# A new instruction order for a fused attention and feed-forward layer

## The chip, the cores and the metric

The kernel runs on one core of one Trainium2 chip. Such a core has five engines, each with an instruction queue of its own that it works through in order: TensorE (PE in the profile) multiplies matrices, VectorE (DVE), ScalarE (ACT) and GpSimd (POOL) work element by element, and SyncE (SP) here only issues DMAs. ScalarE issues some DMAs too, from the same queue as its arithmetic. Matrix products land in PSUM, eight banks of 512 fp32 columns, and are copied out ("evacuated") by VectorE or ScalarE.

The metric is the time on the device, in microseconds (us), median of the runs shown.

## The reference

One pre-norm transformer layer over 2048 tokens of width 640, with 32 heads of 20. Attention goes in four segments of 512 tokens: each segment has causal softmax attention within itself, and a linear memory of the segments before it, mixed by a gate from beta. A feed-forward part of width 1728 with silu follows.

```python
for s in range(N):                      # N = 4 segments of L = 512
    qs, ks, vs = q[:, :, s], k[:, :, s], v[:, :, s]
    p = softmax(qs @ ks.T * scale + mask)
    a_dot = p @ vs
    a_mem = (phi(qs) @ M) / (phi(qs) @ z + 1e-06)
    outs.append(g * a_mem + (1 - g) * a_dot)
    M, z = M + phi(ks).T @ vs, z + phi(ks).sum()
h = x + concat(outs) @ wo               # q, k, v from layernorm(x)
out = h + silu(layernorm(h) @ w1) @ w2
```

Here phi(t) is t + 1 for positive t, and exp(t) otherwise.

## The kernel before

The program is a graph of many small tasks. `ORDER`, a list of names, gives the order in which they are emitted; `schedule` (L287) reads it. An entry such as `n1_st3/A:0,0` is a task, the engine that it goes to (A ScalarE, D VectorE, G GpSimd, S SyncE, where the task may go to more than one) and the buffer slots that it takes. The list is the outcome of a search over a model of the chip; the model's costs are not in the program. Each engine gets its own tasks in the order of the list, so the list is five queue orders at once; waits between engines are worked out from the data (`Tracker.add`, L91).

Every task name has a stage and numbers. In the order of the data, for segment s, 128-token block b (four a segment), head group g of four heads and chunk c of 128 columns:

- `x0`, `x1`, `x2` (blocks 2 and 3), `x4` (blocks 4 to 7), `x8` (8 to 11), `x12`: loads of the tokens (L579). `w_q`, `w_k0`, `w_k1`, `w_wv0`, `w_wv1`, `w_wo`, `w_w1_*`, `w_w2_*`: loads of the weights (L582); `beta` (L594).
- `n1_st`, `n1_r`, `n1_ap`: layer norm of a block, as statistics (L747, L750; on ScalarE L739, L742), one over the deviation (an addition, L762 on VectorE or L765 on GpSimd, then a power on GpSimd, L768) and application (L774). In segment 0 `n1_tp` transposes on TensorE (L783) and `n1_te` evacuates (L792); later `n1_tr` is a transposing DMA (L798). `n2_*` is the second layer norm.
- `re_wq`, `re_wk`: copies that put the query and key weights' columns in order (L699).
- `pr` (L861): query (w = 0) and key (w = 1) projections of chunk c, in segment 0 in two halves x and y; `qe` evacuates them (L869 on ScalarE, L870 on VectorE). `ex` (L876), `pha` (L883) and `phb` (L889) make phi.
- `vt` (L901): twelve small DMAs a segment that move parts of the chunks 0 to 4 to other partitions, for the head groups 5 to 7. They are issued from SP and ScalarE.
- `v` (L826) and `ve` (L836, L837): values. `qk` (L938): scores of four heads; `e` (L949): their exponential on ScalarE; `mk` (L960): the causal mask of a diagonal block, on GpSimd.
- `av` (L981): scores times values; `oe` (L994, L996): evacuation; `tn` (L1010, L1014): memory part and transpose; `nm` (L1027 to L1047): normalization; `ad` (L1055): sum. `kt` (L1095), `mz` (L1103), `ma`, `mb` (L1129 to L1139): the memory.
- `ot` (L1156), `wo` (L1164), `rs` (L1172): output projection and residual. `h1` (L1193, L1199), `th` (L1208), `s` (L1214): the first feed-forward product and silu; `h2` (L1241), `o` (L1254), `out` (L1259): the second product, residual and store.
- `zpad` is a tile of zeros, `sel` the identity (L633, from `iota`), `w2z` and `vpad0`, `vpad1` are memsets on GpSimd, `mt`, `mta`, `mtb`, `mm`, `mzc` small constants there. `fill36` is 36 matmuls on zeros without use for the result (L619), and needs `zpad`. `zf0` and `lsc0` read beta on ScalarE.

Of the kernel before, what the change touches and what calls it, by code (L numbers as in the profile page):

```python
# [371 lines left out]
mk3x_256 phb041 vt04/S vt05/S vt08/S pr010y:6 pr020y:7 pha021:1 qe010y/D lsc2 qe020y/D pr011y:5 qe011y/D lsc3 pr000y:4  # L372
qe000y/D n1_st11:2 ex021:0 phb021 n1_r11/D qk4x0:0 e4x2:5 v00:6 e4x0 mk4x_0 ve00/D:0 n1_st9:1 n1_ap5:0 mk4x_256
n1_r9/D vt03/A n1_ap11:1 vt00/S vt09/S qk0yb0:2 e0yb2:4 v01:0 e0yb0 mk0yb_0 vt06/A ve01/A ex011:2 mk0yb_256 vt010/S
n1_tr5 n1_tr4 kt00:1 kt02:0 n1_tr7 w_w1_1 v03:6 ve03/D qk1yb0:2 e1yb0:6 av0x:0 av2x:1 oe0x/D:1 av4x:6 oe2x/D:0 e1yb2
mk1yb_0 mk1yb_256 tn0x:7 nm0x:0 n1_st10:0 n1_r10/D oe4x/A:1 n1_ap9:0 qk7x0:0 v02:4 e7x2:2 e7x0 mk7x_0 tn4x:7 mk7x_256
ve02/A av1x:6 oe1x/D:1 n1_ap10:2 qk5x0:0 e5x0:0 e5x2 mk5x_0 nm4x:0 v11:4 pha011:2 phb011 qk6x0:0 mk5x_256 ve11/D:1
tn2x:7 av7x:6 ex031:0 e6x2:1 oe7x/D:0 tn1x:4 e6x0 mk6x_0 mk6x_256 nm1x:3 fill2:5 av3x:5 nm2x:1 tn7x:6 nm7x:2 oe3x/A:1
qk0ya0:0 e0ya2:5 av5x:4 oe5x/D:0 mz00:5 ma00/D:0 mb00:0 tn3x:7 nm3x:1 e0ya0 av6x:6 qk1ya0:2 kt04:1 e1ya2:0 oe6x/D:1
tn5x:7 nm5x:3 tn6x:6 nm6x:0 pha031:1 phb031 ot1:0 n1_st8:6 ot0 e1ya0 n1_r8/G v10:0 ve10/A qk2ya0:4 e2ya0:2 av0y:3  # L380
oe0y/D:1 mz02:2 ma02/D:3 v12:0 e2ya2 qk2yb0:2 e2yb0:1 mb02:0 w_w2_0/A e2yb2 mk2yb_0 ve12/D wo1:6 qk3ya0:0 e3ya2:3
kt01:0 rs1 mk2yb_256 n2_st1:5 n2_r1/G wo0:4 tn0y:6 nm0y:1 rs0 e3ya0 n2_ap1:3 n2_tr1:0 av1y:7 oe1y/A:0 qk4ya0:0 pr101:6
v13:4 e4ya2:4 e4ya0 qe101/D:0 n2_st0:3 n2_r0/G ve13/D pha101:2 n2_ap0:3 n2_tr0 ex101:2 phb101 qk3yb0:0 e3yb2:5 pr120:7
qe120/D:0 e3yb0 mk3yb_0 mk3yb_256 qk4yb0:2 e4yb0:0 e4yb2 mk4yb_0 av2y:6 oe2y/D:1 mk4yb_256 w_w2_1/S ex120:0 pr100:0
qe100/D qk5ya0:2 e5ya2:2 tn2y:6 nm2y:2 e5ya0 pr121:1 pha120:0 phb120 qk5yb0:4 e5yb0:6 qe121/D pha121:0 e5yb2 n1_ap8:3
pr141:0 qe141/D:0 qk6ya0:1 h1_0_7_0:5 av3y:6 tn1y:7 mk5yb_0 pha100:0 nm1y:1 e6ya0:1 th0_7_0:0 s0_7_0:0 oe3y/D:1
h1_0_5_0:0 e6ya2 th0_5_0:1 h1_0_12_0:1 th0_12_0:0 qk7ya0:2 e7ya2:3 mk5yb_256 av5y:7 s0_5_0 s0_12_0 oe5y/D:0 mz01:6
e7ya0 tn3y:0 ma01/D:2 mb01:0 nm3y:0 kt03:0 h1_0_4_0:1 qk6yb0:4 e6yb2:5 e6yb0 mk6yb_0 mk6yb_256 pr110:0 qe110/D:0
th0_4_0:0 ex100:1 h1_0_3_0:2 s0_4_0 pha110:0 th0_3_0:1 s0_3_0 phb100 qk7yb0:4 w_w2_2/S w_w2_3/S e7yb2:2 av4y:3
oe4y/D:1 e7yb0 mk7yb_0 ex121:2 pr140:0 qe140/D h1_0_1_0:1 th0_1_0:1 mk7yb_256 pha140:0 s0_1_0 qk8a0:2 e8a0:6 tn4y:6  # L390
# [926 lines left out]
```

## Time and profile before

| | |
|---|---|
| Median of 3 runs | 301.52 us (301.2 to 302.24) |
| The profiled execution | 302.09 us, its span 300.4 us |
| TensorE busy | 288.8 us, 96% of the span |
| VectorE busy | 222.4 us, 74% |
| ScalarE busy | 223.1 us, 74% |
| GpSimd busy | 142.7 us, 48% |
| DMA | 24.66 MB |

Lines of the profile name a source line, an engine and an operation, then `out<-in` with sizes and a count. In a view in order of time the first two numbers are start and duration in us, and brackets hold the idle time before and what ended it. `PEld` is the load of a matmul's weights, which overlaps; a `q` after an engine is its queue at work on a DMA issue. In a group, the numbers behind the bar are busy us, mean ns of one, and idle us before. A row of stretches has busy us and count by engine, the granted clock, the DMA engines' share and GB/s. DMA rows have size, and us from issue to landing; q1 is the hardware queue that SP feeds, q10 ScalarE's. Matmul durations overlap, so TensorE's busy time is not its work.

### The profile page before, as it was taken

Reading aid. Unit: us, or ns where it says so; the run is one execution under the profiler, and the core shown is the slowest. Engines: PE = TensorE matmul, PEld = TensorE weight load, DVE = VectorE, ACT = ScalarE, POOL = GpSimd, SP = SyncE. Lnnn points to the kernel's source line nnn. Section 1 sums busy time; section 2 is a strip of 40 time slices with the busy share of each in tenths; the row PEclk is TensorE's granted clock in tenths of the full one; section 3 lists DMA queues with packets and bytes.
Section 4 is the critical chain, followed back from the end, with each engine's and each line's share of the span. In section 5 each row is a group of like instructions: output and inputs, shape, how many; then the busy total and the mean of one; then the engine's idle time right before and its main releaser. Section 6 shows DMA issues by size and latency. Waiting matters only on the chain.

```text
span 300.4 us, 7527 instructions
## 1 busy us (share of the span) xinstructions
PE 288.8 (96%) x2999; PEld 171.4 (57%) x3023; DVE 222.4 (74%) x515; ACT 223.1 (74%) x318; POOL 142.7 (48%) x272
## 2 busy tenths in 40 slices
...
GB/s 256 362 350 77 116 117 126 89 56 135 85 88 102 63 2 19 42 95 23 94 138 44 79 9 20 39 85 78 47 65 24 2 44 68 46 86 23 0 9 81
DMA packets 49250, 24.66 MB, mean 82 GB/s; under 512 B 39168, under 2 KB 47616, under 8 KB 49216
## 3 DMA queue, kind: packets, MB, share of 16 engines
...
q14 instruction: 10, 0.08, 0.1%
...
## 4 chain that ended last, share of the span: by engine, by line
PE 77%; DVE 12%; DMA 4%; ACT 3%; issue 2%; SPq 0%; POOL 0%; DVEq 0%; ACTq 0%
PE ps_all L1241 21%; PE ps_all L1199 16%; PE ps_all L861 9%; PE ps_all L1164 8%; PE ps_all L938 7%; PE ps_all L981 6%; PE ps_all L826 5%; DMA sT<-in_A_wk_dram 3%; PE ps_all L1010 2%; ACT PT L949 2%; PE ps_all L1014 2%; PE ps_all L1103 2%; DVE stt L747 2%; DMA oT<-otok 1%; DVE on L1047 1%
## 5 line engine op out<-in xcount | busy, mean ns | idle before, releaser
L949 ACT ACTIVATE PT<-ps_all 128x1024 bf16<-128x1024 f32 (+1 forms) x168 | 157.0, 992 | 15.2 <-PE ps_all L938 13.6
L960 POOL TENSOR_SCALAR_AFFINE_SELECT PT<-PT 128x512 bf16<-128x512 bf16 x128 | 82.7, 649 | 66.9 <-ACT PT L949 63.4
L1241 PE MATMUL ps_all<-w_sb,sT 128*128 128x320 bf16 (+2 forms) x462 | 65.1, 295 | 0.0
L1199 PE MATMUL ps_all<-hT,w_sb 128*128 128x512 bf16 (+1 forms) x314 | 61.6, 335 | 1.5 <-DVE sT L1214 0.4
L1208 ACT ACTIVATE th<-ps_all 128x512 f32<-128x512 f32 (+2 forms) x70 | 34.9, 517 | 36.1 <-PE ps_all L1199 27.4
L1241 PEld LDWEIGHTS ps_all<-w_sb,sT 128*128 128x128 bf16 x462 | 43.3, 98 | 18.9 <-issue 2.1
L1214 DVE SCALAR_TENSOR_TENSOR sT<-th,ps_all 128x512 bf16<-128x512 f32 (+2 forms) x70 | 37.8, 558 | 14.9 <-ACT th L1208 14.2
L1199 PEld LDWEIGHTS ps_all<-hT,w_sb 128*128 128x128 bf16 x325 | 29.6, 98 | 24.9 <-issue 2.8
L1254 DVE SCALAR_TENSOR_TENSOR x_tok<-ps_all,x_tok 128x640 bf16<-128x640 f32 (+3 forms) x18 | 13.3, 748 | 22.4 <-PE ps_all L1241 22.3
L747 DVE BATCH_NORM_STATS2 stt<-x_tok 128x6 f32<-128x320 bf16 x62 | 27.1, 479 | 2.3 <-DMA x_tok<-in_A_x_dram 2.0
L768 POOL TENSOR_TENSOR rst<-rst,eps_c 128x1 f32<-128x1 f32 x32 | 18.3, 573 | 15.4 <-DVE rst L762 13.6
L1164 PE MATMUL ps_all<-wo_sb,oT 128*128 128x320 bf16 x160 | 24.1, 300 | 0.2
L1055 POOL TENSOR_TENSOR otok<-on 128x320 bf16<-128x320 bf16 x24 | 19.0, 799 | 11.0 <-DVE on L1047 11.0
L981 PE MATMUL ps_all<-PT,Vx 128*32 128x256 bf16 (+3 forms) x576 | 23.5, 287 | 0.7 <-DVE Vx L837 0.3
L1047 DVE TENSOR_TENSOR on<-ps_all,rd 128x640 bf16<-128x640 f32 x24 | 19.8, 824 | 0.8
L1164 PEld LDWEIGHTS ps_all<-wo_sb,oT 128*128 128x128 bf16 x160 | 14.8, 98 | 7.8 <-issue 2.0
L870 DVE CAST QK<-ps_all 128x512 bf16<-128x512 f32 x23 | 15.7, 685 | 4.7 <-PE ps_all L861 4.3
L996 DVE TENSOR_SCALAR oTs<-ps_all,lsc 128x512 bf16<-128x512 f32 (+1 forms) x28 | 17.0, 618 | 2.2 <-PE ps_all L981 2.1
L826 PE MATMUL ps_all<-wv_sb,xT 128*128 128x320 bf16 x120 | 18.3, 299 | 0.3 <-ACT Vx L836 0.3
L981 PEld LDWEIGHTS ps_all<-PT,Vx 128*32 128x32 bf16 x576 | 12.2, 96 | 11.1 <-issue 5.1
L774 DVE TENSOR_SCALAR xn_rot<-x_tok,mvt,rst 128x640 bf16<-128x640 bf16 x32 | 15.2, 477 | 4.1 <-POOL rst L768 3.5
L861 PE MATMUL ps_all<-xT,wqr 128*128 128x512 bf16 x69 | 17.2, 379 | 0.7 <-DVE otok L1029 0.2
...
## 6 DMA issues: line engine op xcount, KB each, us to landing
...
x_tok<-in_A_x_dram SPq DMA_DIRECT2D x2, 640.0 KB, 11.5
...
```

The source lines that it names most:

```text
L747: T.add(DV, lambda e, hh=hh: e.bn_stats(out=stt[:, s, 6 * hh:6 * hh + 6], in_=xb[:, 320 * hh:320 * hh + 320]), reads=R((xa, xsub)), writes ...
L826: fns.append(lambda e, c=c, hh=hh: e.matmul(bank(ps, hh)[:, 0:320], lhsT=xT_[:, c, 128 * i:128 * i + 128], rhs=wv_sb[:, c, 320 * hh:320 * ...
L861: fns = [lambda e, kc=kc: e.matmul(bank(ps)[:, lo:hi], lhsT=wt[:, kc, c, :], rhs=xT_[:, kc, lo:hi], start=(kc == 0), stop=(kc == NC - 1)) ...
L949: T.add(AC, lambda e: e.activation(out=pt[:, pta.slot, q0:q0 + 2, 0:width], in_=sc3[:, b0:b0 + 2, 0:width], func=ACT.Exp, scale=SCALE), re ...
L960: T.add(PO, lambda e: e.affine_select(out=v, in_=v, pattern=[[0, 4], [1, 128]], compare_op=ALU.is_ge, fill=0.0, base=0, channel_multiplier ...
L981: fns.append(lambda e, j=j, r=r, h=h, pa=pa, pt=pt, co=co, q0=q0, ji=ji: e.matmul(bank(po)[32 * r:32 * r + 32, q0:hi], lhsT=Vx[:, vx.slot, ...
L1047: T.add(DV, lambda e: e.tensor_tensor(out=on[:, ona.slot, :, :].rearrange("p b (x e) -> p b x e", e=DH), in0=v[:, :, :, 0:DH], in1=r2.unsq ...
L1164: fns.append(lambda e, c=c, hh=hh: e.matmul(bank(ps, hh)[:, 0:320], lhsT=oT[:, c, 128 * i:128 * i + 128], rhs=wo_sb[:, c, 320 * hh:320 * h ...
L1199: fns = [lambda e, c=c: e.matmul(bank(ps)[:, lo:hi], lhsT=w1_sb[:, c, 128 * f:128 * f + 128], rhs=hT[:, c, lo:hi], start=(c == 0), stop=(c ...
L1208: T.add(AC, lambda e: e.activation(out=th[:, tha.slot, lo:hi], in_=bank(ps)[:, lo:hi], func=ACT.Tanh, scale=0.5), reads=R((ps, [0])), writ ...
L1214: T.add(DV, lambda e: e.scalar_tensor_tensor(out=sT[:, f, lo:hi], in0=th[:, tha.slot, lo:hi], scalar=1.0, in1=bank(ps)[:, lo:hi], op0=ALU. ...
L1241: fns.append(lambda e, f=f, t0=t0, fr=fr, hh=hh, n=n: e.matmul(bank(pa, hh)[:, 0:n], lhsT=sT[:, f, t0:t0 + 128], rhs=w2_sb[:, fr, c0 + 320 ...
```

## The change

`ORDER` is replaced by another list over the same tasks, with the same count except the fillers. Engines change for 27 tasks:

| from, to | tasks |
|---|---|
| ScalarE to VectorE | qe031x, qe030y, qe030x, oe4x, qe300, qe301, oe22, oe25, oe27 |
| VectorE to ScalarE | qe041x, qe041y, qe310, qe341, oe26 |
| GpSimd to VectorE (the addition of n1_r or n2_r) | n1_r6, n1_r4, n1_r15, n2_r8 |
| VectorE to GpSimd (the same) | n1_r9, n1_r10, n2_r2, n2_r4 |
| SP to ScalarE (DMA issue) | x8, out1, out4, out6, out13 |

The list is one line longer, so line numbers of the profile after are higher by one. The parts of the lists that the prediction speaks of:

```diff
 ORDER = """
-halfc:0 epsc iota mt2 x1:3 vpad1 zpad sel w2z/G:0 x0:7 w_q:0 epsg0 mt0 mta0 x2:5,0 w_k1 w_k0 w_wv1:0 warm n1_st3/A:0,0
-n1_st0/D:1 n1_st1/D:6 mtb0 mm0 n1_r0/G n1_r1/D n1_ap0:0 n1_ap1:1 n1_st2/D:2 mm2 n1_r2/D re_wq0/D:0 re_wq2/D n1_r3/G
-w_wv0 x4:1,2,4,6 w_wo:0 beta w_w2_4 w_w1_2:0 mt3 mta2 mtb2 w_w1_3 w_w2_5 vpad0 n1_ap2:3 mta3 mm7 x8/S:8,9,10,11 mm6
-re_wq1/D mt1 mta1 mtb1 mm3 mm5 mtb3 mm11 mm1 n1_ap3:2 re_wk0/D:0 re_wk2/D re_wk4/D mm8 re_wq3/D re_wk3/D mm10 re_wq4/D
-n1_st6:5 mm4 n1_r6/G w_w1_4 w_w1_0 n1_st7:4 fill36:0 n1_st4:7 n1_r7/G n1_r4/G mm9 n1_tp1:0 n1_tp0:2 fill12:7 n1_tp2:6
...
-pr001y:5 qe001y/A pha001:2 pr031y:0 qe031y/A:0 qk1x0:1 e1x2:1 e1x0 mk1x_0 mk1x_256 zf0 zf1 mzc8 mzc2 mzc7 lsc0 mzc10
-mzc5 mzc1 pr030y:7 lsc1 mzc9 pr031x:6 qe031x/A pr041x:5 qe041x/D:0 mzc3 mzc0 mzc11 mzc4 qe030y/A ex001:1 mzc6 epsg1
-n1_ap4:2 pr041y:0 qk2x0:1 e2x2:2 pr030x:6 qe030x/A pr040y:7 e2x0 mk2x_0 mk2x_256 pr040x:5 qe041y/D phb001 pha041:0
-ex041:2 qe040y/D qe040x/D vt011/S:0 pr021y:4 qe021y/A n1_st5:3 n1_r5/G qk3x0:0 e3x0:3 vt02/A e3x2 vt01/S mk3x_0 vt07/A
...
-ad14 pha210:0 pha221:0 pr241:7 qe241/A:0 h1_0_12_1:6 phb210 th0_12_1:1 s0_12_1 qk16b0:0 e16b0:2 tn12:4 nm12:0,1
-h1_0_4_1:7 th0_4_1:0 s0_4_1 phb201 e16b2 ad12 h1_0_0_1:6 th0_0_1:1 h1_0_10_1:1 th0_10_1:0 s0_10_1 s0_0_1 av15:0
-oe15/A:0 ex221:2 phb221 kt22:0 qk16a0:2 e16a2:6 e16a0 mk16b_0 mk16b_384 h1_0_6_1:7 th0_6_1:0 tn15:0 ex220:0 mb12:0
...
-vt22/S vt21/S phb220 qk17b0:0 e17b0:3 e17b2 mk17b_0 vt27/S vt24/S pha230:0 mk17b_384 phb240 phb231 h1_0_13_1:5
...
-ma14 mb14:0 ad18 h1_1_10_0:6 th1_10_0:0 s1_10_0:0 x12/A tn16:4 qk21b0:0 h1_1_4_0:7 nm16:2,1 e21b0:6 pha241:0 ad16
-e21b2 th1_4_0:0 mk21b_0 s1_4_0 h1_1_7_0:6 th1_7_0:1 s1_7_0 phb241 mk21b_384 qk20a0:2 e20a2:0 e20a0 mk20a_0 h1_1_12_0:0
...
-tn23:0 nm23:1,0 mk25a_0 pr341:3 e24b0:0 qe341/D:0 pha330:0 mb23:0 e24b2 mk24b_0 mk24b_384 pha320:0 ad23 phb320 ex310:1
...
-v31:0 mz24:2 h1_1_13_0:3 th1_13_0:0 qk25b0:4 e25b0:2 ve31/D ma24 s1_13_0 e25b2 mk25b_0 mk25b_384 mb24:0 pha340:0
...
-h1_2_5_0:0 th2_5_0:1 ot15:0 s2_5_0 ot13 h1_2_8_0:7 th2_8_0:1 h1_2_9_0:1 th2_9_0:0 h2_8_0:2 s2_8_0 s2_9_0 h1_2_11_0:5
-ot14 th2_11_0:0 s2_11_0 wo15:6 rs15 n2_st15:5 ot12 n2_r15/D n2_ap15:1 h2_8_1 h2_8_2 wo13:0 rs13 n2_st13:4 wo14:4 rs14
-n2_st14:0 n2_r13/G n2_r14/G n2_tr15:0 n2_ap13:3 n2_tr13 n2_ap14:2 n2_tr14 h2_9_0:6 h2_9_1 wo12:0 h2_8_3 rs12 n2_st12:7
-n2_r12/D n2_ap12:0 h2_10_0:4 o8 h2_9_2 h2_9_3 n2_tr12 o9 out9/A out8/A h2_10_1 h2_10_2 h2_10_3 h2_11_0:0 h2_11_1
-h2_11_2 h2_11_3 o10 o11 out11/A h1_3_4_0:5 h1_3_13_0:7 th3_4_0:1 th3_13_0:0 s3_4_0:0 s3_13_0 h1_3_3_0:6 th3_3_0:1
-s3_3_0 h1_3_5_0:3 th3_5_0:0 h1_3_2_0:2 th3_2_0:1 s3_5_0 s3_2_0 h1_3_0_0:4 th3_0_0:1 h1_3_12_0:1 th3_12_0:0 s3_12_0
...
+x1:3 iota:0 sel x0:7 mt1 mt0 mta0 w_q:0 mtb0 mm2 mm0 mm9 mt3 epsc x2:5,0 w_k1 halfc w_k0 w_wv0:0 zpad mt2 mta2 mtb2
+w_wv1 mm4 warm n1_st0/D:1,0 n1_r0/G x4:1,2,4,6 w_wo:0 beta n1_st1/D:6 n1_r1/D n1_ap0:0 n1_ap1:1 n1_st2/D:2 n1_r2/D
+n1_st3/A:0 n1_r3/G mm7 w2z/G:0 w_w2_4 w_w1_4:0 w_w1_0 re_wq2/D:0 mta3 mta1 mtb1 x8/A:8,9,10,11 mm1 mm5 mm3 mtb3 w_w1_3
+w_w2_5 w_w1_2 re_wq0/D mm11 mm8 mm10 n1_ap2:3 vpad0 re_wq1/D re_wk0/D:0 n1_ap3:2 re_wk2/D mm6 re_wk4/D fill25:0
+re_wk3/D re_wq4/D n1_st4:7 n1_st6:5 re_wq3/D n1_r6/D n1_r4/D n1_st7:4 n1_r7/G epsg0 vpad1 n1_tp0:3 n1_te0/A:0 n1_tp1:5
+fill24:1 n1_te1/A re_wk1/A n1_tp2:0 pr000x:2 n1_te2/A pr010x:4 qe010x/A:0 qe000x/A:0 pr001x:3 qe001x/A n1_ap6:1
+n1_tr6:0 n1_tp3:6 n1_te3/A pr021x:5 qe021x/A:0 qk0x0:0 e0x0:0 n1_ap4:2 pr011x:4 pr020x:6 pr001y:7 qe011x/A e0x2
+qe020x/A mk0x_0 mk0x_256 qe001y/A pr031y:5 qe031y/A:0 qk1x0:1 e1x0:1 e1x2 zf0 pha001:2 zf1 mzc7 mzc0 mzc9 mzc1 mzc3
+mk1x_0 mzc11 mzc4 mzc5 mzc10 mzc8 pr041y:0 mzc6 qe041y/A:0 mzc2 pr041x:6 mk1x_256 pr031x:7 qe031x/D epsg1 lsc0 lsc1
+qe041x/A n1_ap7:3 qk2x0:2 e2x2:2 pr030x:1 pr040x:0 e2x0 ex041:2 ex001:1 qe030x/D qe040x/D mk2x_0 pr040y:6 pha041:0
+qe040y/D pr030y:5 qe030y/D vt011/S:0 pr021y:4 qe021y/A qk3x0:0 mk2x_256 e3x0:3 vt02/A e3x2 n1_st5:3 phb041 vt01/S
...
+pr201:5 qe201/A tn10:1 nm10:0,0 pha200:0 phb200 h1_0_7_1:0 th0_7_1:0 pha201:1 qk15a0:3 e15a2:3 s0_7_1 pr221:7 av14:1
+e15a0 mk15a_0 oe14/D:0 qe221/A pha221:0 ex201:2 ad10 av12:6 oe12/D:1 ad13 qk15b0:2 e15b2:4 vt23/S:0 tn14:0 nm14:3,0
...
+qk16b0:0 e16b0:2 tn12:4 nm12:0,1 h1_0_4_1:7 th0_4_1:0 s0_4_1 phb201 e16b2 mk16b_0 h1_0_0_1:6 th0_0_1:1 h1_0_10_1:0
+th0_10_1:0 s0_10_1 av15:1 oe15/A:0 phb210 s0_0_1 mk16b_384 ex221:2 phb221 kt22:0 qk16a0:2 e16a2:6 ad12 h1_0_6_1:7
...
+mk16e_256 vt28/S v22:6 ve22/D ex220:0 ex240:2 phb231 vt22/S phb240 qk17b0:0 e17b0:3 e17b2 pha220:0 phb220 mk17b_0
...
+e21b0:6 h1_1_4_0:7 pha241:0 h1_1_7_0:6 mb14:0 e21b2 mk21b_0 mk21b_384 th1_4_0:0 s1_4_0 th1_7_0:1 s1_7_0 phb241
...
+e25a0:5 vt36/S:0 e25a2 mk25a_0 vt39/S vt30/S ex310:1 qk24b0:4 tn23:1 pha320:0 ex320:2 e24b0:0 pha330:0 phb320 nm23:1,0
...
+e25b0:2 e25b2 s1_13_0 pha310:0 pha340:0 phb340 phb310 vt34/S mk25b_0 mk25b_384 mk26b_384 mb24:0 h2_4_0:0 h2_4_1
...
+h1_2_5_0:0 th2_5_0:0 h1_2_9_0:1 s2_8_0 s2_5_0 th2_9_0:0 s2_9_0 h1_2_11_0:6 h2_8_0:4 th2_11_0:0 s2_11_0 wo15:2 rs15
+n2_st15:5 n2_r15/D n2_ap15:1 h2_9_0:0 wo14:6 rs14 n2_st14:0 n2_tr15:0 wo13:2 rs13 n2_st13:4 n2_r14/G n2_ap14:2 n2_tr14
+n2_r13/G n2_ap13:3 n2_tr13 h2_9_1 h2_9_2 h2_9_3 wo12:6 rs12 n2_st12:7 n2_r12/D n2_ap12:0 n2_tr12 o9 out9/A h2_8_1
+h2_8_2 h2_8_3 o8 out8/A h2_11_0:2 h2_11_1 h2_11_2 h2_11_3 h2_10_0:6 o11 h2_10_1 h2_10_2 h2_10_3 o10 out10/A out11/A
+h1_3_12_0:2 h1_3_13_0:0 th3_13_0:0 th3_12_0:1 s3_12_0:0 h1_3_4_0:3 th3_4_0:1 s3_13_0 s3_4_0 h1_3_1_0:4 h1_3_0_0:1
...
```

158 lines of the change are left out of this document (79 added, 79 removed).

## The prediction

> **What bounds the kernel now.** I read the page's busy shares and chain first, then a table of stretches, then the start in order of time, then the DMA rows.
>
> ```profile
> span 300.4 us, 7527 instructions
> PE 288.8 (96%) x2999; PEld 171.4 (57%) x3023; DVE 222.4 (74%) x515; ACT 223.1 (74%) x318; POOL 142.7 (48%) x272
> ...
> PE 77%; DVE 12%; DMA 4%; ACT 3%; issue 2%; SPq 0%; POOL 0%; DVEq 0%; ACTq 0%
> ```
>
> TensorE is 96% busy and is 77% of the chain that ended last, so the first guess is that nothing else matters. The stretches say otherwise:
>
> ```profile
> core 0: us, PE busy (x) PEld busy (x) DVE busy (x) ACT busy (x) POOL busy (x), PEclk, DMA share, GB/s
> 10.00:20.00 10.00, 9.08 (x99) 6.90 (x100) 9.57 (x37) 9.46 (x24) 8.52 (x30) 1.00 1.05 354
> 20.00:33.00 13.00, 12.15 (x143) 8.12 (x141) 12.79 (x39) 11.58 (x19) 12.25 (x30) 1.00 0.77 142
> 33.00:48.00 15.00, 14.11 (x199) 8.21 (x200) 12.29 (x38) 14.31 (x19) 7.73 (x13) 1.00 0.57 134
> 48.00:89.00 41.00, 39.79 (x497) 22.61 (x494) 30.31 (x80) 40.35 (x61) 17.55 (x29) 1.00 0.43 90
> 89.00:97.00 8.00, 7.95 (x87) 4.28 (x88) 7.68 (x17) 6.57 (x8) 4.68 (x8) 1.00 0.37 85
> 97.00:143.00 46.00, 44.90 (x518) 26.42 (x519) 39.55 (x89) 43.93 (x64) 27.74 (x45) 1.00 0.23 42
> 143.00:240.00 97.00, 95.64 (x1022) 52.53 (x1032) 71.08 (x147) 81.16 (x102) 53.55 (x89) 1.00 0.28 56
> ```
>
> From 10 to 33 us VectorE is the full engine (9.57 of 10, 12.79 of 13). From 33 to 89 ScalarE is (14.31 of 15, 40.35 of 41). Only from 143 us on has everything but TensorE room. So a microsecond lost before 33 us is handed to ScalarE, which has 1.3 us to spare until 89, and then to TensorE, which has 0.05 of 8 at 89 to 97 and 1.4 of 97 after 143. A delay in the start is therefore nearly permanent, and a gain in the second half can be at most its small idle time.
>
> **The change, step by step.** No instruction is added or removed, except one 256-column filler of the start; TensorE's work is the same and in nearly the same order. What moves is queue order, 14 PSUM evacuations and 8 small layer-norm steps to another engine, and five DMA issues (x8, out1, out4, out6, out13) from SP's queue to ScalarE's.
>
> *1. x8 on ScalarE's queue: the term that I think decides.* Before, x8 (four blocks, 640 KB) is issued last of the big loads, behind x4 and the weights on SP's queue. After, it stands on ScalarE's queue just behind n1_st3.
>
> ```profile
> 2.81 0.56 SPq L579 DMA_DIRECT2D x_tok<-in_A_x_dram  x1
> 3.41 3.40 SPq L582 DMA_DIRECT2D wo_sb<-in_A_wo_dram  x1
> ```
> ```profile
> 8.78 0.83 ACT L742 ACTIVATE otok<-x_tok,mvt 128x640 bf16<-128x640 bf16 x1
> ```
> ```profile
> x_tok<-in_A_x_dram SPq DMA_DIRECT2D x1, 640.0 KB, 11.9
> ```
> ```profile
> q1 hardware_dynamic: 616, 0.76, 55.6%
> q10 hardware_dynamic: 589, 0.72, 50.4%
> ```
> ```profile
> q1 hardware_dynamic: 1252, 1.43, 107.7%
> ```
>
> The first DMA row is x4: issued at 2.81, landed 11.9 later, at 14.7. The next two are the queues from 5 to 9 us: SP's (q1) and ScalarE's (q10) share evenly, 0.76 and 0.72 MB in 4 us, 0.18 a microsecond each. The last is 11 to 15 us, when ScalarE's queue is empty: SP's moves 1.43 MB, 0.36 a microsecond. After the change ScalarE's queue gets 0.65 MB more, issued at about 8.8, beside L742. At 0.18 that keeps the sharing up for 3.6 us longer, in which SP's queue loses 3.6 x 0.18 = 0.65 MB, that is 1.8 us at 0.36. x4's bytes are the next but one on SP's queue, so I take 1.6 of the 1.8: x4 lands at 16.3. Bounds: 0 (x4 already through) to 1.8.
>
> Who waits? VectorE's three statistics n1_st4, n1_st6, n1_st7 read x4, and everything on VectorE stands behind them:
>
> ```profile
> 11.53 1.86 DVE L699 COPY wkr<-sT 128x400 bf16<-128x400 bf16 x7
> ```
> ```profile
> 14.83 0.86 DVE L747 BATCH_NORM_STATS2 stt<-x_tok 128x6 f32<-128x320 bf16 x2
> ```
> ```profile
> 18.52 0.28 DVE L883 TENSOR_SCALAR phiK<-w_sb 128x512 bf16<-128x512 bf16 x1
> ...
> 19.24 0.77 DVE L774 TENSOR_SCALAR xn_rot<-x_tok,mvt,rst 128x640 bf16<-128x640 bf16 x1
> ...
> 20.73 0.72 DVE L883 TENSOR_SCALAR phiK<-w_sb 128x512 bf16<-128x512 bf16 x1
> 21.36 0.74 DVE L870 CAST w_sb<-ps_all 128x256 bf16<-128x256 f32 x2
> ```
>
> ```profile
> 19.18 2.83 POOL L960 TENSOR_SCALAR_AFFINE_SELECT PT<-PT 128x512 bf16<-128x512 bf16 x4
> ```
> ```profile
> L774 DVE TENSOR_SCALAR xn_rot<-x_tok,mvt,rst 128x640 bf16<-128x640 bf16 x32 | 15.2, 477 | 4.1 <-POOL rst L768 3.5 <-ACT hT L792 0.2
> ```
>
> The first of them starts at 14.83, 0.1 after the landing: there is no margin. In the new list VectorE arrives at 15.1 (n1_ap3 slides behind re_wk0, a step of 0.48 at the mean; re_wq3's three copies slide behind the statistics, -0.4 as a share of the seven key copies in 1.86; a long memset now meets the first key copy, +0.2, an estimate). So the statistics start at 16.3, 1.5 late. Beta, behind x4 on SP's queue, and zf0 on ScalarE, which reads it, come later by the same 1.8; this is not added, since the next gate holds ScalarE longer.
>
> *2. The gate of the shifted heads.* The DMAs vt01 to vt011 need all query and key chunks 3 and 4. Their last evacuation is qe040x before, ending at 22.1 (the row 21.36 above), and qe030y after. From the first statistic to that point the new list has on VectorE: re_wq3 +0.4, n1_r6 and n1_r4 +0.3, three evacuations of 0.41 against two, less their overlap +0.35, phb001 moved behind -0.5; sum +0.6. Against it, collisions: the 0.77 and 0.72 above stand beside four GpSimd masks (19.18 to 22.01), while such steps take 0.48 at the mean and 0.28 in the row before, and the new list puts n1_ap4 ahead of the masks; -0.3 (of up to -0.75). So the gate opens 1.5 + 0.6 - 0.3 = 1.8 late.
>
> ```profile
> 22.20 7.28 SPq L901 DMA_DIRECT2D w_sb<-w_sb  x8
> ```
> ```profile
> 22.20 0.84 ACT L949 ACTIVATE PT<-ps_all 128x768 bf16<-128x768 f32 x1
> 22.21 1.44 ACTq L901 DMA_DIRECT2D w_sb<-w_sb  x1
> 23.70 0.81 ACT L949 ACTIVATE PT<-ps_all 128x768 bf16<-128x768 f32 x1 [0.65 <-DVE mvt L750]
> ```
> ```profile
> 31.28 0.47 ACT L994 ACTIVATE oTs<-ps_all,lsc 128x256 bf16<-128x256 f32 x1
> ```
>
> SP's eight issues start at 22.20, right at the gate. ScalarE's vt02 stands between two exponentials, and the second (23.70) waits until it is issued; so ScalarE itself is held 1.8. It gets 0.47 back where oe4x (31.28) leaves for VectorE. At 33 us ScalarE and TensorE are then 1.3 late; the SP chain ends at 31.3 instead of 29.5 and, with an unseen landing time, holds qk7x0 between 0.5 and 1.8. I take +1.4.
>
> *3. From 33 to 143 us.* Same order on ScalarE. out1's issue there costs nothing, because it goes out beside a running instruction, as 22.21 beside 22.20; without that cover, about 0.5. The gain to look for is collisions:
>
> ```profile
> L883 DVE TENSOR_SCALAR phiK<-QK x10: 283/290/745, 52.3 to 156.6; 128x512 bf16<-128x512 bf16 x10
> ```
>
> A step at 290 at the median and 745 at worst loses 0.45. The new list moves pha221, phb201, pha241, phb241, pha340, phb220 and phb320 away from masks, seven times 0.45, about 3 us of VectorE time. But VectorE idles 6.4 of the 46 us at 97 to 143, and TensorE only 1.1. So the gain is between 0 and 1.1, and I take 0.3.
>
> The Trainium skill's page "SBUF — State Buffer", "Who interferes with whom", says that a VectorE copy or tensor_scalar in a two-port mode and a GpSimd instruction take turns, the later one blocked to the end of the other. The row 19.24 agrees: 0.77 beside a mask. By it each of the seven steps, once clear, gains all of its excess, step 3 could stand at its upper end of 1.1, and the sum would be +0.3 instead of +1.1; that is near the rival "relief" below.
>
> *4. Second half and tail.* Eight evacuations and the rest of the issues move; VectorE gets two of them more (five come, three go) from 143 to 240, where it idles 26. Cost 0, 0.5 if one lands ahead of a step that TensorE waits for. The last segment's order is new: h1_3 now stands behind 76 matmuls after wo12 instead of 78.
>
> ```profile
> 257.30 10.60 PE ps_all L1241 x78
> ```
> ```profile
> 261.53 1.20 SPq L798 DMA_TRANSPOSE hT<-xn_rot  x1
> ```
>
> The cover shrinks by 2 x 0.136 = 0.3; the last transpose is issued at 261.53 and TensorE comes to it at 267.9, so 0. The closing groups are the same.
>
> **Sum.** +1.4 - 0.3 = +1.1. The profiled execution took 302.09 (its span and 1.7 around it); it becomes 303.2. That execution lies 0.57 over the median of 301.52, so the forecast for the median is 302.6.
>
> **The rivals.** *No change:* x4 is through before x8's packets start, or its delay is shorter than VectorE's own later arrival (0.3). Then the gate moves 0.3 + 0.6 - 0.3, which oe4x's 0.47 and step 3's 0.3 outweigh by 0.2: 301.3. For it: an SP issue was held 3.40 at 3.41, so a queue's share is not only packets. Against: the even split in the rows.
>
> *Relief, faster:* the start neutral, and the collisions' 1.1 all on the path: 301.52 - 1.1 = 300.4. It decides if x4 lands by 15.1 and if TensorE's idle at 97 to 143 halves. For it: VectorE is 12% of the chain. Against: ScalarE is as full there (43.93 of 46), and masks don't hold it.
>
> *Late fillers, slower still:* zpad's memset now stands behind sel on VectorE, and the fillers that keep TensorE running before its first data need it.
>
> ```profile
> 0.00:5.00 5.00, 3.89 (x23) 2.90 (x24) 3.45 (x7) 1.49 (x2) 3.63 (x17) 1.00 0.62 201
> ```
> ```profile
> 1.11 4.09 PE L619 MATMUL ps_all<-zpad 128*128 128x256 bf16 x23 [1.11 <-DVE zpad L596]
> ...
> 1.22 1.88 DVE L633 TENSOR_SCALAR ident<-iot 128x128 bf16<-128x128 int32 x1 [0.17 <-POOL iot L631]
> ```
> ```profile
> 10.48 0.45 PE L783 MATMUL ps_all<-ident,xn_rot 128*128 128x128 bf16 x5 [1.26 <-DVE xn_rot L774]
> ```
>
> The first 23 fillers took 4.09, 0.18 each, with the granted clock at 1.00. If sel is held again for 1.88, behind GpSimd's first steps, zpad comes at 3.1; 25 fillers at 0.18 end at 7.6, the two transposes behind them at 8, and if the 24 that follow keep that pace they end at 12.3, where the third transpose ran at 10.48: 1.8 late, TensorE and ScalarE with it. This hides for the most part under x4's 1.5; where half is paid on top of the forecast, 303.6. It decides from 0.10 a filler upwards, where the 24 end at 10.5. The page "TensorE: Matmul & The Clock Gate" of the Trainium skill, "Part 1", says the array starts at half clock and needs about 3.4 us of matmuls for the full one; the slow first fillers agree with that, the granted clock does not show it.
>
> **How the numbers follow.** Forecast (302.0 to 303.6 by the bounds of steps 1 to 3) 0.50; no change 0.18; relief 0.22; late fillers 0.10. 0.3% is 0.9 us, about what a measurement of this kernel tells from none. The forecast's own lower part (302.0 to 302.4) counts as no change, 0.08. So slower 0.52, same 0.26, faster 0.22. The range takes in relief, down to where oe4x's 0.47 is won there as well (299.9), and the late fillers with most of their 1.8 paid: 300.0 to 304.0.
>
> **What would show it.** Right: the wait of stt on the x_tok DMA near 15 grows by about 1.2, the eight SP issues start near 24.0, ScalarE's gap at 23.7 moves to 25.5, and 143 to the end is as long as before. Wrong: statistics at 15.1 or earlier, SP issues at 22.5 or earlier, or a stretch after 33 us that is over 1 us shorter.

## The result and the profile after

The changed kernel takes 302.81 us (median of 21 runs, 301.33 to 303.96) against 301.52 (21 runs, 300.98 to 303.1); the ratio is 1.0030, 95% interval 1.0016 to 1.0045. That is 0.9 us slower by the ratio and 1.3 by the medians; 302.6 was forecast. The number came out. The way to it was half right, and the number held partly by luck.

The two profiled executions alone would mislead. That of before took 302.09, 0.57 over its median; that of after took 302.32, 0.49 under its own. Side by side they differ by 0.2 us, where the kernels differ by about 1. So the start is read below over the traces of all runs, not of one pair.

The stretches of after, in the columns of the table of before (length, busy us and count of each engine, clock, DMA):

```profile
span 300.6 us, 7530 instructions
PE 290.5 (97%) x3001; PEld 172.5 (57%) x3024; DVE 222.4 (74%) x519; ACT 220.7 (73%) x314; POOL 142.0 (47%) x272
```
```profile
10.00:20.00 10.00, 9.99 (x111) 7.86 (x109) 9.67 (x37) 9.21 (x22) 7.11 (x23) 1.00 1.06 359
20.00:33.00 13.00, 11.20 (x133) 7.06 (x131) 12.77 (x36) 9.96 (x16) 12.65 (x33) 1.00 0.73 141
...
97.00:143.00 46.00, 45.36 (x521) 26.62 (x524) 38.77 (x91) 44.41 (x64) 28.37 (x46) 1.00 0.26 43
143.00:240.00 97.00, 95.54 (x1016) 52.47 (x1028) 71.86 (x149) 79.31 (x99) 53.07 (x88) 1.00 0.27 56
```

VectorE is as full as before from 10 to 33 us (9.67 of 10, 12.77 of 13). ScalarE has lost 1.6 of busy time at 20 to 33 (9.96 against 11.58). From 97 to 143 TensorE is busier by 0.46 (45.36 against 44.90), a first sign of where the list wins something. The DMA rows from 11 to 15 us are as step 1 said:

```profile
q1 hardware_dynamic: 647, 0.80, 59.3%
q10 hardware_dynamic: 509, 0.65, 47.7%
```

x8 on ScalarE's queue takes 0.65 MB of that stretch, and SP's queue moves 0.80 MB where it moved 1.43. But x4 is not as late as forecast. Issued at 2.81, it lands 12.1 us later, at 14.9, not at 16.3:

```profile
x_tok<-in_A_x_dram SPq DMA_DIRECT2D x1, 640.0 KB, 12.1
```

The statistics start right behind the landing, at 14.93. They do wait for x4, but no idle time is shown, because VectorE's copies before them (first row below) are still on record until 15.03. SP's issues at the gate start at 22.60, not at 24.0.

```profile
13.78 1.25 DVE L700 COPY wqr<-sT 128x400 bf16<-128x400 bf16 x3
14.93 0.89 DVE L748 BATCH_NORM_STATS2 stt<-x_tok 128x6 f32<-128x320 bf16 x2
```
```profile
22.60 1.64 SPq L902 DMA_DIRECT2D w_sb<-w_sb  x2
```

### The profile page after: what moved, and what is told of

Read it like the earlier page. It is cut to its first block, busy times and chain, and to the rows that moved or that the text cites. A ratio compares the mean times of both kernels' runs of the same rounds, so it can differ in the third digit from the quotient of the medians.

```text
span 300.6 us, 7530 instructions
## 1 busy us (share of the span) xinstructions
PE 290.5 (97%) x3001; PEld 172.5 (57%) x3024; DVE 222.4 (74%) x519; ACT 220.7 (73%) x314; POOL 142.0 (47%) x272
## 4 chain that ended last, share of the span: by engine, by line
PE 76%; DVE 12%; ACT 5%; DMA 2%; issue 2%; POOL 1%; DVEq 0%; ACTq 0%
PE ps_all L1242 20%; PE ps_all L1200 16%; PE ps_all L862 9%; PE ps_all L1165 8%; PE ps_all L939 7%; PE ps_all L982 6%; PE ps_all L827 5%; ACT PT L950 4%; DVE stt L748 3%; PE ps_all L1011 2%; PE ps_all L1104 2%; PE ps_all L1015 2%; DMA oT<-otok 1%; DVE on L1048 1%; DMA x_tok<-in_A_x_dram 1%
## 5 line engine op out<-in xcount | busy, mean ns | idle before, releaser
L961 POOL TENSOR_SCALAR_AFFINE_SELECT PT<-PT 128x512 bf16<-128x512 bf16 x128 | 81.6, 645 | 61.5 <-ACT PT L950 58.9
L1200 PE MATMUL ps_all<-hT,w_sb 128*128 128x512 bf16 (+1 forms) x315 | 60.8, 336 | 0.8 <-issue 0.3
L1215 DVE SCALAR_TENSOR_TENSOR sT<-th,ps_all 128x512 bf16<-128x512 f32 (+2 forms) x70 | 38.0, 560 | 14.3 <-ACT th L1209 13.4
L1255 DVE SCALAR_TENSOR_TENSOR x_tok<-ps_all,x_tok 128x640 bf16<-128x640 f32 (+3 forms) x18 | 13.3, 747 | 21.7 <-PE ps_all L1242 21.7
L1056 POOL TENSOR_TENSOR otok<-on 128x320 bf16<-128x320 bf16 x24 | 19.2, 802 | 12.1 <-DVE on L1048 12.1
L997 DVE TENSOR_SCALAR oTs<-ps_all,lsc 128x512 bf16<-128x512 f32 (+1 forms) x31 | 19.0, 625 | 2.3 <-PE ps_all L982 2.0
L862 PE MATMUL ps_all<-xT,wkr 128*128 128x512 bf16 x69 | 17.4, 380 | 0.5 <-issue 0.3
```

What stands on the lines that cost most here:

```text
L862: fns = [lambda e, kc=kc: e.matmul(bank(ps)[:, lo:hi], lhsT=wt[:, kc, c, :], rhs=xT_[:, kc, lo:hi], start=(kc == 0), stop=(kc == NC - 1)) ...
L961: T.add(PO, lambda e: e.affine_select(out=v, in_=v, pattern=[[0, 4], [1, 128]], compare_op=ALU.is_ge, fill=0.0, base=0, channel_multiplier ...
L1200: fns = [lambda e, c=c: e.matmul(bank(ps)[:, lo:hi], lhsT=w1_sb[:, c, 128 * f:128 * f + 128], rhs=hT[:, c, lo:hi], start=(c == 0), stop=(c ...
L1215: T.add(DV, lambda e: e.scalar_tensor_tensor(out=sT[:, f, lo:hi], in0=th[:, tha.slot, lo:hi], scalar=1.0, in1=bank(ps)[:, lo:hi], op0=ALU. ...
```

## The experiments

Times are medians; the ratio to before, with its interval, is what the verdicts use, because the runs of before that stand beside each group vary from 301.33 to 301.54.

**1 and 2. Start and rest, crossed.** At about 36 us both lists have emitted the same tasks, but for n1_ap10. So one list's start can be joined to the other's rest. The first lines behind the joint:

```diff
 qk6x0:0 mk5x_256 ve11/D:1 tn2x:7 av7x:6 ex031:0
-e6x2:1 oe7x/D:0 tn1x:4 e6x0 mk6x_0 mk6x_256 nm1x:3 fill2:5
+oe7x/D:0 fill2:4 e6x2:1 e6x0 nm2x:1 mk6x_0 mk6x_256 tn1x:4
...
```
```diff
 qk6x0:0 ve11/D:1 mk5x_256 ex031:0 tn2x:7 av7x:6
-oe7x/D:0 fill2:4 e6x2:1 e6x0 nm2x:1 mk6x_0 mk6x_256 tn1x:4
+n1_ap10:2 e6x2:1 oe7x/D:0 tn1x:4 e6x0 mk6x_0 mk6x_256 nm1x:3 fill2:5
...
```

> The list of before up to ex031 (about 36 us of the span), the rest of after. The two halves hold the same tasks, n1_ap10 apart, which the new rest brings a little earlier or later. Theory S (the change loses its time in the start, before 36 us): as fast as before or up to 0.3 us faster, 301.2 to 301.6. Rival R (the loss is in the rest of the list, and the start is neutral): as slow as after, 302.4 to 302.8.

> The list of after up to av7x (about 36 us), the rest of before: the mirror image. Theory S: as slow as after or up to 0.3 slower, 302.6 to 303.1. Rival R: as fast as before, 301.3 to 301.7. If the two parts add, the sum of the changes of this run and of the one with the other start equals that of the whole change, +0.9 to +1.3.

Measured: start of before with rest of after 300.87, ratio 0.9972 (0.9954 to 0.9990); start of after with rest of before 303.26, ratio 1.0072 (1.0046 to 1.0098). Theory S holds, and more than it said: the new start costs 0.58% (1.0030 against 0.9972), 1.7 us, and 0.72%, 2.2 us, with the other rest; the new rest gains 0.28% to 0.42%, 0.8 to 1.3 us. The two runs add up to +0.44%, 1.3 us, where the whole change has +0.30% (0.16% to 0.45%). The first of the two kernels is faster than both lists.

**3 and 4. x8, undone and alone.**

```diff
-n1_st3/A:0 n1_r3/G mm7 w2z/G:0 w_w2_4 w_w1_4:0 w_w1_0 re_wq2/D:0 mta3 mta1 mtb1 x8/A:8,9,10,11 mm1 mm5 mm3 mtb3 w_w1_3
-w_w2_5 w_w1_2 re_wq0/D mm11 mm8 mm10 n1_ap2:3 vpad0 re_wq1/D re_wk0/D:0 n1_ap3:2 re_wk2/D mm6 re_wk4/D fill25:0
+n1_st3/A:0 n1_r3/G mm7 w2z/G:0 w_w2_4 w_w1_4:0 w_w1_0 re_wq2/D:0 mta3 mta1 mtb1 mm1 mm5 mm3 mtb3 w_w1_3
+w_w2_5 x8/S:8,9,10,11 w_w1_2 re_wq0/D mm11 mm8 mm10 n1_ap2:3 vpad0 re_wq1/D re_wk0/D:0 n1_ap3:2 re_wk2/D mm6 re_wk4/D fill25:0
```

> After, with x8 back on SP's queue, fifth of the weight loads there as before. Step 1 of the prediction (x8's packets take half the bandwidth from x4, and the statistics wait 1.5 us): 1.3 to 1.5 us faster than after, about 301.4, and the statistics no earlier than VectorE's arrival at about 14.9. Rival (the bytes are shared, but x4 is through in time and VectorE arrives no earlier): within 0.3 of after, 302.5 to 302.9, and the first statistic again at about 14.9.

```diff
-halfc:0 epsc iota mt2 x1:3 vpad1 zpad sel w2z/G:0 x0:7 w_q:0 epsg0 mt0 mta0 x2:5,0 w_k1 w_k0 w_wv1:0 warm n1_st3/A:0,0
+halfc:0 epsc iota mt2 x1:3 vpad1 zpad sel w2z/G:0 x0:7 w_q:0 epsg0 mt0 mta0 x2:5,0 w_k1 w_k0 w_wv1:0 warm n1_st3/A:0,0 x8/A:8,9,10,11
...
-w_wv0 x4:1,2,4,6 w_wo:0 beta w_w2_4 w_w1_2:0 mt3 mta2 mtb2 w_w1_3 w_w2_5 vpad0 n1_ap2:3 mta3 mm7 x8/S:8,9,10,11 mm6
+w_wv0 x4:1,2,4,6 w_wo:0 beta w_w2_4 w_w1_2:0 mt3 mta2 mtb2 w_w1_3 w_w2_5 vpad0 n1_ap2:3 mta3 mm7 mm6
```

> Before, with x8 alone moved to ScalarE's queue behind n1_st3. Step 1 of the prediction: the first of the three statistics starts 1.3 to 1.6 us late (16.1 to 16.4 in place of 14.8) and the time is 302.6 to 303.0. Rival: the statistics start within 0.3 of 14.8, and the time is 301.3 to 301.8.

Measured: after with x8 on SP 301.19, ratio 0.9999 (0.9981 to 1.0018); before with x8 on ScalarE 302.77, ratio 1.0050 (1.0031 to 1.0070). So x8 alone costs 0.5%, 1.5 us, in the old list, and 0.31%, 0.9 us, in the new one. Its price is near the one forecast. What waits is another matter: the statistics start at 14.61, not at 16.1 to 16.4. The rows of before with x8 alone moved, VectorE first:

```profile
13.37 0.59 DVE L699 COPY wqr<-sT 128x400 bf16<-128x400 bf16 x3
14.61 0.89 DVE L747 BATCH_NORM_STATS2 stt<-x_tok 128x6 f32<-128x320 bf16 x2 [0.65 <-DMA x_tok<-in_A_x_dram]
...
19.26 0.59 DVE L650 TENSOR_SCALAR zf<-zf 128x32 f32<-128x32 f32 x1 [0.65 <-ACT zf L648]
```
```profile
19.00 0.23 ACT L648 ACTIVATE zf<-beta_bc 128x32 f32<-128x32 bf16 x1 [1.25 <-DMA beta_bc<-in_A_beta_dram]
```

VectorE waits 0.65 for x4, and in this trace that is forgotten 4 us later: ScalarE stands 1.25 us before zf0, which reads beta, and VectorE's zf1 waits for zf0. In this run beta lands 13.4 us after its issue, in the run with before's start 10.6:

```profile
wo_sb<-in_A_wo_dram SPq DMA_DIRECT2D x1, 800.0 KB, 15.4
...
beta_bc<-in_A_beta_dram SPq DMA_DIRECT2D x1, 8.0 KB, 13.4
```
```profile
wo_sb<-in_A_wo_dram SPq DMA_DIRECT2D x1, 800.0 KB, 12.6
beta_bc<-in_A_beta_dram SPq DMA_DIRECT2D x1, 8.0 KB, 10.6
```

Beta is 8 KB, but it is issued behind the 800 KB of wo and lands right behind them. The new start with the old rest shows the same wait on ScalarE:

```profile
19.06 0.23 ACT L649 ACTIVATE zf<-beta_bc 128x32 f32<-128x32 bf16 x1 [1.28 <-DMA beta_bc<-in_A_beta_dram]
```

The profiled execution of after had it at 18.07 with 0.14 of waiting, so its trace hides part of the loss.

**5 and 6. Late x8, early x4.** If x8 costs by what it takes from loads still flowing, an x8 issued later on the same queue must cost nothing; and if VectorE's wait for x4 is the price, an earlier x4 must win it back.

```diff
-n1_tr6:0 n1_tp3:5 pr021x:0 qk0x0:1 pr011x:7 n1_te3/A qe021x/A:0 e0x0:0 qe011x/A e0x2 mk0x_0 mk0x_256 pr020x:6 qe020x/A
+n1_tr6:0 n1_tp3:5 pr021x:0 qk0x0:1 pr011x:7 n1_te3/A x8/A:8,9,10,11 qe021x/A:0 e0x0:0 qe011x/A e0x2 mk0x_0 mk0x_256 pr020x:6 qe020x/A
```

> Before, with x8 on ScalarE's queue again, but issued behind n1_te3 (about 13.7 us), when x4's bytes are through (12.6 us in the runs with x8 on SP's queue). Theory X (x8 costs because its packets take bandwidth from x4 while x4 still flows): nothing is left of the 1.4, the time is 301.0 to 301.6, and the first of the three statistics starts as in before's list with x8 on SP, 13.9 to 14.8. Rival Q (the issue on ScalarE's queue, or the loss of x8 on SP's queue, costs by itself): 302.4 to 302.9 again.

```diff
-x1:3 iota:0 sel x0:7 mt1 mt0 mta0 w_q:0 mtb0 mm2 mm0 mm9 mt3 epsc x2:5,0 w_k1 halfc w_k0 w_wv0:0 zpad mt2 mta2 mtb2
-w_wv1 mm4 warm n1_st0/D:1,0 n1_r0/G x4:1,2,4,6 w_wo:0 beta n1_st1/D:6 n1_r1/D n1_ap0:0 n1_ap1:1 n1_st2/D:2 n1_r2/D
+x1:3 iota:0 sel x0:7 mt1 mt0 mta0 w_q:0 mtb0 mm2 mm0 mm9 mt3 epsc x2:5,0 w_k1 halfc w_k0 x4:1,2,4,6 w_wv0:0 zpad mt2 mta2 mtb2
+w_wv1 mm4 warm n1_st0/D:1,0 n1_r0/G w_wo:0 beta n1_st1/D:6 n1_r1/D n1_ap0:0 n1_ap1:1 n1_st2/D:2 n1_r2/D
```

> After, x8 left on ScalarE's queue, but x4 issued on SP's queue ahead of the 480 KB of w_wv0, which nothing needs before v00 at 25 us. Theory X (VectorE waits for x4): x4's bytes are through some 1.3 us or more earlier (12.5 or less in place of 13.9), and the time falls by 1.2 to 1.6, to about 301.2 to 301.6. Rival B (x8 costs through beta, the weights or something else behind x4 on SP's queue): the time stays at 302.5 to 302.9.

Measured: late x8 301.57, ratio 1.0001 (0.9983 to 1.0020): theory X. The queue costs nothing, the time of the issue does. Early x4 303.00, ratio 1.0035 (1.0017 to 1.0053): theory X fails. x4 lands at 12.0, the statistics start at 14.20 with no wait, and the time does not move; beta is still behind:

```profile
19.05 0.23 ACT L649 ACTIVATE zf<-beta_bc 128x32 f32<-128x32 bf16 x1 [1.22 <-DMA beta_bc<-in_A_beta_dram]
```

**7 and 8. Early beta, in both lists.**

```diff
-x1:3 iota:0 sel x0:7 mt1 mt0 mta0 w_q:0 mtb0 mm2 mm0 mm9 mt3 epsc x2:5,0 w_k1 halfc w_k0 w_wv0:0 zpad mt2 mta2 mtb2
-w_wv1 mm4 warm n1_st0/D:1,0 n1_r0/G x4:1,2,4,6 w_wo:0 beta n1_st1/D:6 n1_r1/D n1_ap0:0 n1_ap1:1 n1_st2/D:2 n1_r2/D
+x1:3 iota:0 sel x0:7 mt1 mt0 mta0 w_q:0 mtb0 mm2 mm0 mm9 mt3 epsc x2:5,0 w_k1 halfc w_k0 w_wv0:0 beta zpad mt2 mta2
+mtb2 w_wv1 mm4 warm n1_st0/D:1,0 n1_r0/G x4:1,2,4,6 w_wo:0 n1_st1/D:6 n1_r1/D n1_ap0:0 n1_ap1:1 n1_st2/D:2 n1_r2/D
```

> After, x8 left on ScalarE's queue, but the 8 KB load of beta issued on SP's queue behind w_wv0, ahead of x4 and w_wo. In the runs with x8 on ScalarE's queue beta lands at 18.1 to 19.0, with x8 on SP's at 16.0 to 17.7, and in three of four of the former ScalarE idles 1.2 us before zf0, which reads it. Theory Beta (the start's loss is this wait): no idle time before zf0, the gate at 22.0 to 22.6, and 1.2 to 1.6 us less than after: 301.2 to 301.6. Rival X4 (VectorE's wait for x4, or the shared bandwidth in general): 302.4 to 303.0.

The second is experiment 4 with the same step:

```diff
-w_wv0 x4:1,2,4,6 w_wo:0 beta w_w2_4
+w_wv0 beta x4:1,2,4,6 w_wo:0 w_w2_4
```

> Before with x8 on ScalarE's queue behind n1_st3 (302.8 alone), and beta ahead of x4 on SP's. What is left of the 1.4 is the wait for x4: in the run with x8 alone VectorE idled 0.65 us for it at 14.0. Theory Beta: 0.65 of the 1.4 stays at most, 301.4 to 302.1, and VectorE still idles 0.4 to 0.9 before the first of the three statistics. Rival X4: 302.5 to 303.0, with the idle time before zf0 gone.

Measured: 303.98, ratio 1.0079 (1.0051 to 1.0106), and 303.40, ratio 1.0076 (1.0048 to 1.0104). Neither theory's number: both are slower, not faster. The wait for beta is gone (zf0 at 17.65 and 17.50, no idle time), and x4 has taken its place. In the first VectorE waits 0.23 for it at 15.09, in the second 1.50:

```profile
15.09 0.89 DVE L748 BATCH_NORM_STATS2 stt<-x_tok 128x6 f32<-128x320 bf16 x2 [0.23 <-DMA x_tok<-in_A_x_dram]
```
```profile
15.32 0.89 DVE L747 BATCH_NORM_STATS2 stt<-x_tok 128x6 f32<-128x320 bf16 x2 [1.50 <-DMA x_tok<-in_A_x_dram]
```

So x8 delays two loads that the start waits for, x4 (landing at about 15) and beta (at about 19), and where one was moved ahead, the wait for the other stayed. Part of x4's lateness here is its own issue, which stands behind beta's and comes at 3.51 and 3.63 in place of 2.81. That each of the two loads binds is read from the traces; no time shows it, since neither move won anything, and both moved ahead of the weights at once was not tried. Why early beta is slower than after as well (by about 0.5%) is open: the profiled execution of the first, 302.33, is the fastest of its six and shows no loss.

**9. The memsets.** In the trace of after the last query copies, re_wq4, take 1.25 (row 13.78 above; 0.66 in before) while GpSimd fills vpad0, and re_wk0 takes 1.47 (1.04) beside w2z. This run is experiment 3's kernel with the memsets earlier.

```diff
-n1_st3/A:0 n1_r3/G mm7 w2z/G:0 w_w2_4
+n1_st3/A:0 n1_r3/G mm7 w_w2_4
...
-w_wv1 mm4 warm n1_st0/D:1,0 n1_r0/G x4:1,2,4,6 w_wo:0 beta n1_st1/D:6 n1_r1/D n1_ap0:0
+w_wv1 mm4 w2z/G:0 warm n1_st0/D:1,0 n1_r0/G x4:1,2,4,6 w_wo:0 beta n1_st1/D:6 n1_r1/D vpad0 vpad1 n1_ap0:0
...
-mm11 mm8 mm10 n1_ap2:3 vpad0 re_wq1/D
+mm11 mm8 mm10 n1_ap2:3 re_wq1/D
...
-n1_r7/G epsg0 vpad1 n1_tp0:3
+n1_r7/G epsg0 n1_tp0:3
...
```

> After with x8 on SP's queue (301.2), and GpSimd's memsets w2z, vpad0 and vpad1 moved ahead, to where VectorE has no key copies. In after's trace two of VectorE's groups of key and query copies are stretched beside them: re_wk0 takes 1.47 us (1.04 in before) and re_wq4 1.24 (0.66). Theory M (what is left of the start's loss, 0.3, is these collisions): re_wk0 and re_wq4 fall to about 1.0 and 0.7 and the time to 300.4 to 300.9. Rival P (it is the engine placements and their order): 301.0 to 301.4.

Measured: 301.92, ratio 1.0012 (0.9992 to 1.0031), not faster than experiment 3, and neither theory's number. The copies did shrink (0.47 and 0.62), and the collision moved with the memsets. VectorE and GpSimd in that run:

```profile
5.97 0.44 DVE L775 TENSOR_SCALAR xn_rot<-x_tok,mvt,rst 128x640 bf16<-128x640 bf16 x1
6.86 1.41 DVE L775 TENSOR_SCALAR xn_rot<-x_tok,mvt,rst 128x640 bf16<-128x640 bf16 x1 [0.45 <-POOL rst L769]
...
10.94 0.47 DVE L700 COPY wkr<-sT 128x400 bf16<-128x400 bf16 x2
...
13.12 0.62 DVE L700 COPY wqr<-sT 128x400 bf16<-128x400 bf16 x3
```
```profile
6.77 0.66 POOL L627 MEMSET Vx<- 128x128 bf16 x1
7.02 0.45 POOL L628 MEMSET Vx<- 128x48 bf16 x1
7.24 0.81 POOL L627 MEMSET Vx<- 128x128 bf16 x1
```

The same step takes 0.44 alone and 1.41 beside the memsets, and n1_ap1 is a step that TensorE's second transpose waits for; the third transpose then runs at 11.23, where it runs at 10.32 in experiment 3. So the run says how dear such a collision is, 0.97 us, and leaves open whether the start's remaining loss is theirs.

**10 and 11. The gain at 120 us.** In every trace with the new rest ScalarE needs 3.81 to 3.82 us from e16b0 to e16a2, in every trace with the old rest as it was 4.40 to 4.41. Before, two steps of 0.74 and 0.76 (pha221, phb210), slowed beside GpSimd's masks and its memory step mb, stand ahead of s0_12_1 on VectorE, s0_12_1 ends at 120.73, and TensorE's h1_0_0_1, which takes its bank, starts at 120.78. After, there is no such stop:

```profile
118.97 0.74 DVE L883 TENSOR_SCALAR phiK<-QK 128x512 bf16<-128x512 bf16 x1
119.64 0.76 DVE L889 TENSOR_TENSOR phiQ<-phiQ,ex 128x512 bf16<-128x512 bf16 x1
120.32 0.41 DVE L1214 SCALAR_TENSOR_TENSOR sT<-th,ps_all 128x256 bf16<-128x256 f32 x1
```
```profile
120.78 1.26 PE L1199 MATMUL ps_all<-hT,w_sb 128*128 128x256 bf16 x10 [0.41 <-DVE sT L1214]
```
```profile
120.14 1.80 PE L1200 MATMUL ps_all<-hT,w_sb 128*128 128x256 bf16 x15
```

Experiment 10 moves only these two steps, in the list of before:

```diff
-ad14 pha210:0 pha221:0 pr241:7 qe241/A:0 h1_0_12_1:6 phb210 th0_12_1:1 s0_12_1 qk16b0:0
+ad14 pha210:0 pr241:7 qe241/A:0 h1_0_12_1:6 th0_12_1:1 s0_12_1 pha221:0 phb210 qk16b0:0
```

> Before, with pha221 and phb210 moved behind s0_12_1 on VectorE and nothing else. In before the two take 0.74 and 0.75 us beside GpSimd's masks, s0_12_1 frees a PSUM bank behind them at 120.7, and h1_0_0_1 on TensorE idles 0.69 us for it. Theory G (the gain of the new list behind 36 us is this wait): the idle before h1_0_0_1 falls to 0.25 or less and the time is 0.4 to 0.6 below before, 300.8 to 301.1. Rival (the gain comes from VectorE's relief as a whole): 0 to 0.2 below before, 301.2 to 301.5.

Measured: 302.01, ratio 1.0011 (0.9993 to 1.0030). No gain. The stop before h1_0_0_1 is gone, and e16b0 to e16a2 takes 4.72, longer than ever. VectorE, then ScalarE:

```profile
119.35 0.85 DVE L889 TENSOR_TENSOR phiQ<-phiQ,ex 128x512 bf16<-128x512 bf16 x1
...
121.47 0.41 DVE L1214 SCALAR_TENSOR_TENSOR sT<-th,ps_all 128x256 bf16<-128x256 f32 x1
```
```profile
121.96 0.38 ACT L1208 ACTIVATE th<-ps_all 128x256 f32<-128x256 f32 x1 [0.80 <-issue]
```

phb210 still lies beside a mask, now ahead of s0_4_1; that ends at 121.88 and frees the buffer that th0_10_1 takes at 121.96. One wait was exchanged for another. In the new list pha221 runs 2.9 us ahead of e16b0 (0.28 at 117.09 in after) and phb210 behind s0_10_1, so neither stands ahead of s0_12_1 or s0_4_1. From the start of e16b0 to the end of s0_4_1 is 2.93 to 2.94 us in the traces with the old rest, 3.27 in this run, and 2.29 to 2.30 with the new rest: that is the 0.6. What counts is what stands ahead of these two awaited steps. Behind them a collision costs nothing here: in experiment 3's trace phb210 still takes 0.90 beside GpSimd's steps, and the stretch takes 3.81 as in the others.

```profile
122.76 0.90 DVE L890 TENSOR_TENSOR phiQ<-phiQ,ex 128x512 bf16<-128x512 bf16 x1
```

Experiment 11 takes over the whole stretch:

```diff
 s0_8_1 qk14e0:1 e14e0:1 mz11:7 ma11 tn13:5
-pr201:0 e14e2 mk14e_0 nm13:3,1 tn10:1 nm10:0,0 pha200:0 phb200 qe201/A
+mb10:0 nm13:3,1 e14e2 mk14e_0 mk14e_256 pr201:5 qe201/A tn10:1 nm10:0,0 pha200:0 phb200
...
```

> Before, with the new list's order of one stretch alone: the 149 tasks between tn13 and e17a0, about 112 to 136 us, which are the same tasks in both lists. In the five traces with the new list's rest, e16b0 to e16a2 on ScalarE takes 3.8 us, in the four with the old one 4.4. Theory G: the whole gain behind 36 us lies here, 0.4 to 0.7: 300.8 to 301.2. Rival: it is spread over the rest, and this stretch gives 0 to 0.2: 301.3 to 301.6.

Measured: 302.46, ratio 1.0042 (1.0025 to 1.0059). It did not test what it should. e16b0 to e16a2 is 3.81, as in the new list. But the joint brought a clash: pr201 takes bank 5 in the new list, and tn13 holds bank 5 in the old one, so TensorE waits 1.76 us for VectorE to read it, which neither list does.

```profile
111.53 0.32 PE L1014 MATMUL ps_all<-ident,oTs 128*128 128x84 bf16 x4
113.61 0.59 PE L861 MATMUL ps_all<-xT,wkr 128*128 128x512 bf16 x2 [1.76 <-DVE on L1047]
```

Where the gain lies is shown by the traces, 0.6 in this place. The stretches ahead of it and behind it, from e6x and to the end, differ by under 0.2 us at the median of the traces, and the interval of experiment 1 (0.3 to 1.4 us) holds 0.6; but that it is the whole gain is not shown by a time.

**12. oe4x back on ScalarE.**

```diff
-oe2x/D:0 oe4x/D:1 nm0x:0 n1_st10:0
+oe2x/D:0 oe4x/A:1 nm0x:0 n1_st10:0
```

> After, with oe4x back on ScalarE. By step 2 of the prediction ScalarE gets 0.47 us by oe4x's leaving, so this run is 0.3 to 0.5 slower than after: 303.0 to 303.4. Rival (after's trace: ScalarE idles 0.99 us before e7x0, which waits for ve03 on VectorE by way of av4x, tn0x and qk7x0, so the 0.47 falls into idle time): within 0.2 of after, 302.6 to 303.0, and 0.5 less idle time before e7x0.

Measured: 302.28, ratio 1.0031 (1.0006 to 1.0056), beside after's 1.0030. The interval is 0.75 us to each side, too wide to tell 0.47 from nothing, and the median lies below both theories; the traces say more. Below are after, then this run: the 0.99 of idle time before e7x0 becomes 0.30 and 0.27 around oe4x, so most of oe4x's 0.47 falls into idle time, as the rival said.

```profile
32.52 1.51 ACT L950 ACTIVATE PT<-ps_all 128x768 bf16<-128x768 f32 x2 [0.99 <-PE ps_all L939]
```
```profile
32.79 0.47 ACT L995 ACTIVATE oTs<-ps_all,lsc 128x256 bf16<-128x256 f32 x1 [0.30 <-DVE oTs L997]
33.53 1.51 ACT L950 ACTIVATE PT<-ps_all 128x768 bf16<-128x768 f32 x2 [0.27 <-PE ps_all L939]
```

**The start over all traces**, in us from the start of the span: when x4 lands, when VectorE starts the first of the three statistics, when beta lands, how long ScalarE waits before zf0, when the first vt DMA is issued (the gate), and the first e6x exponential, where the two lists come together again.

| trace | x4 lands | statistics | beta lands | wait, zf0 | gate | e6x |
|---|---|---|---|---|---|---|
| before (profiled) | 14.7 | 14.83 | 17.7 | 0 | 22.20 | 36.06 |
| before's start, after's rest | 13.5 | 13.93 | 16.2 | 0 | 21.45 | 35.30 |
| before, x8 late on ScalarE | 13.4 | 14.21 | 16.1 | 0 | 21.25 | 35.30 |
| before, two steps moved | 13.4 | 14.22 | 16.1 | 0 | 21.27 | 35.19 |
| before, stretch of after | 13.7 | 13.81 | 16.4 | 0 | 21.34 | 35.55 |
| before, x8 early on ScalarE | 14.6 | 14.61 | 19.0 | 1.25 | 23.04 | 37.08 |
| the same, beta early | 15.3 | 15.32 | 12.8 | 0 | 22.69 | 36.70 |
| after, x8 on SP | 14.4 | 14.45 | 17.3 | 0 | 22.12 | 36.24 |
| the same, memsets early | 13.3 | 13.66 | 16.0 | 0 | 22.25 | 36.77 |
| after (profiled) | 14.9 | 14.93 | 18.0 | 0.14 | 22.60 | 36.62 |
| after's start, before's rest | 14.6 | 14.66 | 19.0 | 1.28 | 23.55 | 38.05 |
| after, x4 early | 12.0 | 14.20 | 19.0 | 1.22 | 23.28 | 37.79 |
| after, beta early | 15.1 | 15.09 | 12.7 | 0 | 22.76 | 36.89 |
| after, oe4x on ScalarE | 14.2 | 14.19 | 19.0 | 1.27 | 23.08 | 37.68 |

The trace that the prediction was made from is the odd one of the old starts: 0.5 to 0.9 later at e6x than the four others with x8 on SP or late. There x2 landed late (n1_st3 starts at 7.92, in the other traces at 6.47 to 7.21), x4 with it, and VectorE too.

With x8 early on ScalarE's queue the statistics start within 0.03 us of x4's landing in every trace but the one where x4 itself is early. Three of those six waits show as idle time; in the other three the copies before the statistics are still on record.

One caution. The four executions in which ScalarE waits 1.2 to 1.3 us for beta take 0.2 to 1.8 us more than the medians of their kernels, and after's, with 0.14, takes 0.49 less. So this wait differs between executions, and what it costs at the median is not shown by a run.

## Why the prediction came out

- **Step 1, x8 (+1.5): near in price and right in cause, wrong in how it reaches the gate.** x8 early on ScalarE's queue costs 0.9 to 1.5 us, and nothing when it is issued at 13 us (experiments 3 to 5). That two queues share what one had is also what the Trainium skill's page "DMA: Bandwidth & Descriptors" says, in "Queues, rings and completion order": each DMA engine takes turns between the queues that have work; the rows agree (0.80 and 0.65 MB in 4 us). The delay of x4 was put too high. The text has x4 at 16.3 and "no margin" ahead of the statistics; with x8 early it landed at 14.2 to 14.9, about 1.1 later than in the old start's other traces (13.4 to 13.7), where VectorE came 0.1 to 0.8 behind it. The statistics lose 0.4 to 0.8 by x8 alone (14.61 against 13.81 to 14.22), not 1.5; the missing margin was that of the odd trace. And the step failed at "Beta, behind x4 on SP's queue, and zf0 on ScalarE, which reads it, come later by the same 1.8; this is not added, since the next gate holds ScalarE longer." Beta came 2.6 to 2.9 later by x8 alone (19.0 against 16.1 to 16.4). In four of five traces ScalarE waits 1.2 to 1.3 for it, and this wait reaches VectorE, which the gate waits for, through zf1. By the sign that the text gave itself (statistics at 15.1 or earlier) the mechanism, at the size it named, was wrong. How the price divides between x4 and beta stays open, since removing either wait alone won nothing (experiments 6 to 8).
- **Step 2, the gate (+1.8) and oe4x (-0.47).** By the medians of the traces the new start with x8 early opens the gate at 23.08, the old one with x8 on SP or late at 21.34: 1.7 later, near the 1.8. With x8 back on SP it is still 22.12 against 21.45, 0.7 us. These are single executions, and where the 0.7 comes from is not shown; the sum had +0.6 - 0.3 for placements and collisions and 0.3 for VectorE's later arrival. (In that arrival, 15.1, the -0.4 for three of seven copies in 1.86 would be -0.8; the sum does not use it, since x4 was put later still.) The term -0.47 was wrong by the traces: in after ScalarE waits 0.99 for e7x0's scores, where in before it had waited 0.16. What remains of the start beside x8 is 0.27% (0.9999 against 0.9972), 0.8 us, only just clear of the two intervals; the forecast had -0.1 for it. This part is not explained.
- **Step 3, collisions (-0.3, up to -1.1).** The new rest gains 0.8 to 1.3 us by ratios; 0.6 of it is one place at 120 us. Six of the seven steps did come free, in every trace with the new rest; the seventh, phb241, took 0.42 in both lists. Together they take 2.53 us in place of 4.77, so 2.2 and not "about 3" was there to win. The size was near the upper bound, but the 0.6 is not a sum of excesses: it comes where two steps no longer stand ahead of s0_12_1 and s0_4_1, which ScalarE and TensorE wait for. The Trainium skill's page "SBUF — State Buffer", "Who interferes with whom", by which such steps contend with GpSimd's, would have set the sum at that bound; the runs agree with it in step lengths (0.42 for 0.91; 1.41 for 0.44), and the ratios agree with the bound in time. That two steps alone were not worth a microsecond (experiment 10) agrees with the text's caution that VectorE's gain counts only as far as TensorE idles.
- **Step 4, nothing.** e19b0 to the end takes 156.5 in before and 157.05 in after, 156.5 to 157.0 in the other traces with the new rest, 156.4 to 157.5 in those with the old one: no difference beyond this spread.
- **The sum.** Start +1.4 forecast, +1.7 to +2.2 measured; rest -0.3 forecast, -0.8 to -1.3 measured. Two sizes were too small by about as much, with opposite signs, so +1.1 stood. That is luck, as far as the number goes; that the start loses and the rest wins was forecast.
- **The rivals.** "No change" fell with x8's price. "Relief" was half there: its gain behind 36 us came, and the start took it back. "Late fillers" came only in small: sel took 0.27, not 1.88, and zpad was set at 1.36. The third transpose runs behind the fillers without idle time, at 10.43 in after; before had 10.48, but that is the odd trace, and the old start's others have 9.73 to 9.91. So it is about 0.5 late, not 1.8, and whether that is part of the start's loss was not tried.
